# Sketched linear attention and a Fourier mixing block in one kernel: columns d and 128 - d folded before the row transform

## The chip, the cores and the metric

The kernel runs on one core of one Trainium2 chip. A core has five engines that work side by side: TensorE (PE in the profile; its weight loads are listed as PEld), VectorE (DVE), ScalarE (ACT), GpSimd (POOL) and SyncE (SP, which here only issues transfers, DMAs). The metric is the device time of one execution in microseconds. The profiler's records of one execution span a little less than that time; both are given below.

## The reference, cut to what matters

```python
# batch B = 4, heads H = 4, S = 1088 rows, D = 32, sketch R = 8, DM = H * D = 128
def phi(x):
    a = np.einsum('rd,bhsd->bhsr', S1, x)
    b = np.einsum('rd,bhsd->bhsr', S2, x)
    return np.einsum('bhsi,bhsj->bhsij', a, b).reshape(*x.shape[:-1], r * r)
q_p, k_p = (phi(q), phi(k))
kv = np.einsum('bhsf,bhsd->bhfd', k_p, v)
z = np.sum(k_p, axis=2)
num = np.einsum('bhsf,bhfd->bhsd', q_p, kv)
den = np.einsum('bhsf,bhf->bhs', q_p, z)[..., None] + 1e-06
x = (num / den)                       # then heads side by side: x is [4, 1088, 128]
X = np.fft.fft(x, axis=1)
X = np.fft.fft(X, axis=2)
u = x + np.real(X)
un = (u - mean(u)) / np.sqrt(var(u) + 1e-06)      # over the 128 columns
out = u + np.maximum(un @ w_ch1, 0.0) @ w_ch2     # w_ch1 [128, 512], w_ch2 [512, 128]
```

For the change only the middle matters: the real part of a two-dimensional Fourier transform, over the 1088 rows and then over the 128 columns. With cosine and sine tables C and S it is C x C - S x S.

## The kernel before, in words

The program is a list of named steps. Each step has one engine, a function that emits its instructions, and the things that it reads and writes. A string `ORDER` gives one sequence of all steps, so it fixes the order of every engine's own queue; `ENGINE` moves steps to another engine than their default; `BANK` gives each use of PSUM its bank (8 banks of 512 fp32); `BEHIND` makes a load wait until an earlier transfer has landed; `FILL` puts a number of products of zeros ahead of a PE step (three numbers: fp32 products, bf16 products, bank). Semaphores follow from what is read and written. Step names carry the batch b or the group g.

For each batch b:

- `qT`, `kT` (DVE): transposes of 32x32 blocks. `qf`, `kpr` (PE): sketches of q and k. `qa`, `kab` (ACT) copy one factor out of PSUM, `qp` (DVE) and `kp` (POOL or DVE) multiply. `vc` packs v with a column of ones.
- `kv` (PE, L339): sum over rows of features times v, 36 products that show as 72 instructions, because fp32 takes two passes; `kvz` copies it out. `pnd` (PE, L425): numerators and denominators, again 72 instructions. `den`, `rden` and `x` (DVE, L440) divide; x is written as bf16 in 9 blocks of 128 rows; block 8 holds the rows left over of both halves.
- `eo` (POOL or DVE, L96): sum and difference of rows s and s + 544, 128x512 bf16 each.
- `sC`, `sS` (PE, L453, L461, L462): the row transform with cosines and with sines. Each has 2 products of 273 columns for block 8 and 16 products of 136 or 137 columns; weights are all 128 columns of the folded x. `zC`, `zS` copy them out (128x546 each), `zrC`, `zrS` (128x544) make the mirrored half.
- `mix` (PE, L487, L492) for each half of the rows: u = x (one product with the identity) plus the column transform, for each of 4 blocks of 128 rows one product with the cosine matrix `cd` and one with the sine matrix `sd`. `mixl` (L498, L505) does the left-over rows of two batches, with 32-wide products.

Ten groups g follow (two halves of each batch, and two groups of left-over rows): `bn`, `var` (DVE), `sd` (ACT), `rc` (DVE), `un` give the normalized rows; `xt` is a transposing DMA on SP (groups 7, 8 and 9 use `tr` on PE and a copy `ut` instead); `ph` (PE, L559), `rl` (ACT L566 or DVE L568), `po` (PE, L573), `fin` and `out` are the two layers and the store. The left-over group is stored by four DMAs (`st_last`).

Before all that the tables are made: `c_...` constants, `t_turn`, `l_turn`, `d_turn` (POOL) and `t_ph`, `t_pm`, `l_ph`, `l_pm`, `d_ph`, `d_pm` (DVE) angles of the main table, of the left-over rows and of the columns; `t_sin`, `t_cos`, `l_...`, `d_trig` (ACT); `t_neg` the negated tables.

A product can use a part of the PE array. The profile prints that shape: 128\*128 is the whole array, 128\*64 a half of its columns, 128\*32 a quarter, 32\*64 an eighth.

Of the kernel before, what the change touches and what calls it, by code (L numbers as in the profile page):

```python
# [22 lines left out]
LAST = HALF - 512  # L23
NK = HALF // 2 + 1
NB = NK // 2 + 1
BY_DMA = (0, 1, 2, 3, 4, 5, 6)
TWO = 8
# [24 lines left out]
def program(nc, T, x, bank):  # L52
# [31 lines left out]
    def copy(engine, out, in_):  # L84
        if engine == ACTE:
            nc.scalar.copy(out, in_)  # L86
        elif engine == DVE:
            nc.vector.tensor_copy(out, in_)
        else:
            nc.gpsimd.tensor_copy(out, in_)  # L90

    def memset(engine, t, value):
        (nc.vector if engine == DVE else nc.gpsimd).memset(t, value)

    def tt(engine, out, in0, in1, op):
        (nc.vector if engine == DVE else nc.gpsimd).tensor_tensor(out=out, in0=in0, in1=in1, op=op)  # L96
# [32 lines left out]
    def ld_qt():  # L129
        return [nc.sync.dma_start(view(T("qt_in"), 0, [[D, B * H], [1, D]], 32 * j, 32),  # L130
                                  dram(x["q"], (512 + HALF * j) * D, [[D, 32], [S * D, B * H], [1, D]])) for j in range(2)]
# [41 lines left out]
    def c_rows():  # L173
        v = nc.vector
        pi, pa, sr = T("pi"), T("pa"), T("sr")
        v.tensor_scalar(out=pa[:, 0:1], in0=pi[:], scalar1=31, scalar2=None, op0=ALU.bitwise_and)  # L176
        v.tensor_scalar(out=pa[:, 1:2], in0=pi[:], scalar1=32, scalar2=None, op0=ALU.bitwise_and)
        v.tensor_scalar(out=sr[:, 5:6], in0=pa[:, 0:1], scalar1=512.0, scalar2=None, op0=ALU.add)
        v.tensor_scalar(out=sr[:, 4:5], in0=pa[:, 1:2], scalar1=HALF / 32.0, scalar2=sr[:, 5:6], op0=ALU.mult, op1=ALU.add)
        v.tensor_copy(sr[:, 5:6], pi[:])  # L180
        v.tensor_scalar(out=T("sq")[:, 0:5], in0=sr[:, 0:5], scalar1=1.0 / S, scalar2=None, op0=ALU.mult)
        v.tensor_scalar(out=T("sq")[:, 5:6], in0=sr[:, 5:6], scalar1=1.0 / DM, scalar2=None, op0=ALU.mult)
    add("c_rows", DVE, "iota", "rows", c_rows)

    def turn(ph, i, src, period):

        nc.gpsimd.tensor_scalar(out=ph, in0=src, scalar1=T("sq")[:, i:i + 1], scalar2=MAGIC, op0=ALU.mult, op1=ALU.add)
        nc.gpsimd.tensor_scalar(out=ph, in0=ph, scalar1=-MAGIC, scalar2=-float(period), op0=ALU.add, op1=ALU.mult)

    def rest(ph, i, src):  # L190
        nc.vector.scalar_tensor_tensor(out=ph, in0=src, scalar=T("sr")[:, i:i + 1], in1=ph, op0=ALU.mult, op1=ALU.add)  # L191

    def size(pm, ph):
        nc.vector.tensor_scalar(out=pm.bitcast(I32), in0=ph.bitcast(I32), scalar1=0x7FFFFFFF, scalar2=None, op0=ALU.bitwise_and)
# [42 lines left out]

    def d_trig():
        cos(T("cd")[:], T("dpm")[:], DM)
        sin(T("sd")[:, 0, :], T("dph")[:], DM, -1.0)  # L240
        sin(T("sd")[:, 1, :], T("dph")[:], DM)
    add("d_trig", ACTE, "dphb dpm hpi tabsin", "cd sd", d_trig)
# [65 lines left out]
    def kprod(engine, use, ab, kp, lo, hi):  # L308

        b = [[16, hi - lo], [0, R], [1, R]]  # L310
        tt(engine, view(kp, F * lo, [[F, hi - lo], [R, R], [1, R]]), ps(use, 16 * lo + R, b) if engine == DVE else view(ab, 16 * lo + R, b),
# [14 lines left out]
    def vcopy(b, engine):  # L326
        copy(engine, view(T(f"v{b % 2}"), 0, [[33, H], [33 * H, 8], [1, D]]), view(T(f"v_in{b % 2}"), 0, [[8 * D, H], [D, 8], [1, D]]))
# [116 lines left out]

    def fold(b, engine, w):
        tt(engine, T(f"eo{b % 2}")[:, w], T(f"x{b}")[:, 0:4, :], T(f"x{b}")[:, 4:8, :], (ALU.add, ALU.subtract)[w])

    def srow(b, trig):

        ahead = ((0, -3, -4, 7), (1, 2, -5, -6))[trig]  # L450
        z = f"z{trig}{b}"
        for c in range(2):
            nc.tensor.matmul(ps(z, 512 * c, [[1, NK]]), T(f"x{b}")[:, 8, :], T("tabl")[:, trig, NK * c:NK * c + NK],  # L453
                             start=True, stop=False, skip_group_check=True)
        for c in range(2):
            for t in range(4):
                w = T(f"eo{b % 2}")[:, c, t, :]
                i = ahead[t]
                m = T("tab")[:, 2 * t + trig, NB * c:NB * c + NB - c]
                far = T("tab")[:, i, NB * c + 1 - c:NB * c + NB - c] if i >= 0 else T("neg")[:, -i - 3, NB * c + 1 - c:NB * c + NB - c]  # L460
                nc.tensor.matmul(ps(z, 512 * c, [[1, NB - c]]), w, m, start=False, stop=(t == 3), skip_group_check=True)  # L461
                nc.tensor.matmul(ps(z, 512 * c + NB - c, [[1, NB - 1]]), w, far, start=False, stop=(t == 3),  # L462
                                 skip_group_check=True)

    def zev(b, trig, engine):
        copy(engine, view(T(f"z{b}"), 2 * NK * trig, [[1, 2], [2, NK]]), ps(f"z{trig}{b}", 0, [[512, 2], [1, NK]]))

    def zrev(b, trig, engine):
        copy(engine, view(T(f"zr{b}"), 2 * NK * trig, [[1, HALF]]), view(T(f"z{b}"), 2 * NK * trig + HALF, [[-1, HALF]]))


    def zcol(b, trig, half, first, step, n):

        return view(T(f"z{b}" if half == 0 else f"zr{b}"), 2 * NK * trig + first, [[step, n]])
# [8 lines left out]
    def mix(b, half, g):  # L483
# [5 lines left out]
        for t in range(4):  # L489
            for trig in range(2):  # L490
                w = T("cd")[:] if trig == 0 else T("sd")[:, half, :]
                nc.tensor.matmul(ps(u, ut_at(g, t), [[1, 128]]), zcol(b, trig, half, t, 4, 128), w, start=False, stop=True,  # L492
                                 skip_group_check=True)

    def mixl(i):
# [4 lines left out]
        for b in (2 * i, 2 * i + 1):  # L500
            for half in range(2):
                for trig in range(2):
                    w = T("cd")[:] if trig == 0 else T("sd")[:, half, :]
                    p = 64 * (b % 2) + 32 * half
                    nc.tensor.matmul(ps(u, 0, [[1, 128]], p, 32), zcol(b, trig, half, 512, 1, LAST), w, start=False, stop=True,  # L505
                                     tile_position=(0, p), skip_group_check=True)
# [5 lines left out]
    def var(g, n, engine):  # L512
# [8 lines left out]
        p.tensor_tensor(out=d, in0=st[:, 0:n, 1], in1=st[:, 0:n, 4], op=ALU.subtract)  # L521
# [3 lines left out]
        p.tensor_tensor(out=v, in0=v, in1=d, op=ALU.add)  # L525

# [60 lines left out]
    def st_last(i, g):  # L587
        return [nc.sync.dma_start(dram(x["out"], ((2 * i + j // 2) * S + 512 + HALF * (j % 2)) * DM, [[DM, 32], [1, DM]]),
                                  T(f"ot{g % 4}")[32 * j:32 * j + 32, 0:128]) for j in range(4)]
# [38 lines left out]
    for b in range(B):  # L628
# [12 lines left out]
        for w in range(2):  # L641
            e = eng(f"eo{b}.{w}", POOL)
            add(f"eo{b}.{w}", e, f"x:{b}", f"eo:{b}/{w}", lambda b=b, w=w, e=e: fold(b, e, w))
        for trig, n in ((0, "C"), (1, "S")):
            add(f"s{n}{b}", PE, f"eo:{b}/0 eo:{b}/1 x:{b} tab/S0 tab/S1 tab/C0 tab/C1 neg tabL/{n}",
                f"pz{n}:{b}", lambda b=b, trig=trig: srow(b, trig), f"z{trig}{b}:2")
            e = eng(f"z{n}{b}", ACTE)
            add(f"z{n}{b}", e, f"pz{n}:{b}", f"z{n}:{b}", lambda b=b, trig=trig, e=e: zev(b, trig, e), f"z{trig}{b}:2")
            e = eng(f"zr{n}{b}", POOL)
            add(f"zr{n}{b}", e, f"z{n}:{b}", f"zr{n}:{b}", lambda b=b, trig=trig, e=e: zrev(b, trig, e))  # L650
        for half in range(2):
            mixer(b, half, g, (f"zC:{b} zS:{b}", f"zrC:{b} zrS:{b}")[half] + f" x:{b} idb cd sd")
# [11 lines left out]
    "kk": ([128, 2 * NK], FP32), "pi": ([128, 1], I32), "pa": ([128, 2], I32),  # L664
# [4 lines left out]
    "cd": ([128, DM], BF16), "sd": ([128, 2, DM], BF16),  # L669
# [11 lines left out]
    "x": (4, [128, 9, DM], BF16), "eo": (2, [128, 2, 4, DM], BF16), "z": (4, [128, 2, 2 * NK], BF16), "zr": (4, [128, 2, 2 * NK], BF16),  # L681
# [6 lines left out]
def kernel(  # L688
# [108 lines left out]
```

## Time and profile before

| what | value |
|---|---|
| median of 3 runs | 88.58 us (87.52 to 89.68) |
| time of the profiled execution | 87.8 us |
| span of its records | 86.0 us |
| mean granted TensorE clock | 0.969 |
| busy: PE, DVE, ACT, POOL | 76.1, 63.4, 52.5, 41.0 us |
| moved by DMA | 10.49 MB |

A row of a timeline reads: start and duration in us, engine, line, operation, output <- inputs, shape in the PE array (for PE), shapes of the operands, how many instructions in a row; in brackets the idle time before it and what ended it. Matmuls are pipelined and their ends are modelled, so products overlap in the list; the distance between two starts is what a product costs. A row of groups reads: busy us, mean ns of one, then idle time before them. A row of stages reads: busy us of each engine with the number of its instructions, then the granted clock, the share of the DMA engines and GB/s.

### The profile page before, as it was taken

What the parts mean: (1) busy time and instruction counts of PE and PEld (TensorE: products, weight loads), DVE (VectorE), ACT (ScalarE), POOL (GpSimd) and SP (SyncE); (2) the same over time, 40 slices, a digit from 0 to 9 for tenths busy, and PEclk for the clock granted to TensorE, in tenths of its full rate; (3) what the DMA queues carried; (4) which work ended last, traced back from release to release, by engine and by line L of the source; (5) the groups of instructions that cost most, each with busy time, mean ns of one, the idle gap of its engine ahead of it and who ended that gap; (6) DMA issues with size and microseconds to landing.
All of it is one profiled execution on the core that took longest, in us unless ns stands there. A gap on an engine that the chain in (4) does not pass through costs nothing.

```text
span 86.0 us, 3396 instructions
## 1 busy us (share of the span) xinstructions
PE 76.1 (89%) x1434; PEld 58.1 (68%) x1442; DVE 63.4 (74%) x168; ACT 52.5 (61%) x91; POOL 41.0 (48%) x57
## 2 busy tenths in 40 slices
PE   0999999991999999999999999999999988979530
PEld 0244556791899776879799797987777965757220
DVE  5699999999956999975793577395989537682710
ACT  3413669926826535668966176639659859899510
POOL 7888659997076730499992328037500220000000
PEclk9999999999759999999999999999999999999995
DMA  0889996599687862400003001133060360251413
GB/s 4 226 241 326 272 228 115 161 247 294 218 214 209 278 175 58 134 0 8 0 11 61 0 8 30 39 61 126 1 189 0 76 183 0 71 206 75 182 34 119
DMA packets 16176, 10.49 MB, mean 122 GB/s; under 512 B 6944, under 2 KB 14624, under 8 KB 16160
## 3 DMA queue, kind: packets, MB, share of 16 engines
q1 hardware_dynamic: 15976, 10.13, 42.2%
q8 instruction: 11, 0.18, 0.9%
q10 hardware_dynamic: 184, 0.14, 0.5%
q14 instruction: 5, 0.04, 0.1%
HBM read 7.22 MB, written 2.23 MB: 110 GB/s over the span
## 4 chain that ended last, share of the span: by engine, by line
PE 66%; DVE 23%; issue 3%; ACT 3%; POOL 1%
PE ps L425 12%; PE ps L573 9%; PE ps L339 8%; PE ps L559 7%; PE ps L379 6%; PE ps L492 5%; PE ps L462 4%; PE ps L461 4%; DVE t_ph L191 4%; PE ps L453 3%; PE ps L305 3%; ACT t_ht__158 L566 2%; PE ps L487 2%; DVE t_qT__116 L372 1%; DVE t_ht__157 L568 1%
## 5 line engine op out<-in xcount | busy, mean ns | idle before, releaser
L566 ACT ACTIVATE t_ht__158<-ps 128x1024 bf16<-128x1024 f32 x8 | 8.1, 1023 | 1.8 <-PE ps L462 1.1
L96 POOL TENSOR_TENSOR t_kp__119<-t_ab__117 128x512 f32<-128x512 f32 x6 | 6.3, 1068 | 6.1 <-ACT t_ab__117 L357 6.1
L96 POOL TENSOR_TENSOR t_kp__120<-t_ab__118 128x512 f32<-128x512 f32 x8 | 8.9, 1143 | 0.0
L566 ACT ACTIVATE t_ht__157<-ps 128x1024 bf16<-128x1024 f32 (+1 forms) x7 | 6.7, 962 | 2.0 <-PE ps L559 1.9
L78 PE MATMUL ps<-t_wz 128*128 128x512 f32 x6 | 4.3, 810 | 2.0 <-DVE t_pa L176 2.0
L573 PEld LDWEIGHTS <-t_ht__157 128*128 128x128 bf16 x68 | 3.9, 98 | 2.6 <-DVE t_ht__157 L568 1.1
L573 PE MATMUL ps<-t_w2b,t_ht__157 128*128 128x128 bf16 x68 | 4.8, 220 | 0.9 <-DVE t_ht__157 L568 0.9
L425 PE MATMUL ps<-t_kvz,t_qp__125 128*64 128x66 f32 x128 | 5.5, 261 | 0.0
L425 PEld LDWEIGHTS ps<-t_kvz,t_qp__125 128*64 128x64 f32 x128 | 5.2, 173 | 0.5 <-issue 0.4
L386 ACT COPY t_qa__124<-ps 128x1024 f32<-128x1024 f32 x4 | 4.1, 1013 | 1.9 <-PE ps L379 1.4
L573 PE MATMUL ps<-t_w2b,t_ht__158 128*128 128x128 bf16 x68 | 4.8, 219 | 0.3 <-ACT t_ht__158 L566 0.3
L573 PEld LDWEIGHTS <-t_ht__158 128*128 128x128 bf16 x68 | 4.1, 98 | 1.4 <-DVE t_ht__158 L568 0.5
L386 ACT COPY t_qa__123<-ps 128x1024 f32<-128x1024 f32 x4 | 4.0, 1004 | 1.1 <-PE ps L379 1.1
L90 POOL COPY t_zr__142<-t_z__138 128x544 bf16<-128x544 bf16 x2 | 1.3, 642 | 7.1 <-ACT t_z__138 L86 5.6
L223 POOL TENSOR_SCALAR t_neg<-t_tab 128x1096 bf16<-128x1096 bf16 x1 | 3.0, 3001 | 3.2 <-ACT t_tab L200 3.2
L339 PEld LDWEIGHTS ps<-t_v__122,t_kp__120 128*64 128x64 f32 x128 | 4.2, 141 | 0.4 <-issue 0.4
L379 PE MATMUL ps<-t_qT__116,t_sa 32*64 32x256 f32 x64 | 2.8, 400 | 1.9 <-DVE t_qp__126 L390 1.9
L425 PEld LDWEIGHTS ps<-t_kvz,t_qp__126 128*64 128x64 f32 x128 | 3.9, 137 | 0.8 <-issue 0.8
L339 PEld LDWEIGHTS ps<-t_v__121,t_kp__119 128*64 128x64 f32 x128 | 4.1, 138 | 0.6 <-POOL t_zr__139 L90 0.4
L339 PE MATMUL ps<-t_v__122,t_kp__120 128*64 128x33 f32 x128 | 4.4, 225 | 0.0
L339 PE MATMUL ps<-t_v__121,t_kp__119 128*64 128x33 f32 x128 | 4.3, 224 | 0.0
L461 PE MATMUL ps<-t_tab,t_eo__133 128*128 128x137 bf16 (+1 forms) x32 | 4.3, 223 | 0.0
(257 smaller groups left out, 237.5 us busy)
## 6 DMA issues: line engine op xcount, KB each, us to landing
t_q_in__110<-in_q_dram SPq DMA_DIRECT2D x4, 256.0 KB, 3.4
t_k_in__107<-in_k_dram SPq DMA_DIRECT2D x2, 512.0 KB, 4.6
t_v_in__108<-in_v_dram SPq DMA_DIRECT2D x8, 128.0 KB, 3.4
t_v_in__109<-in_v_dram SPq DMA_DIRECT2D x8, 128.0 KB, 3.4
t_k_in__106<-in_k_dram SPq DMA_DIRECT2D x2, 256.0 KB, 4.7
t_q_in__111<-in_q_dram SPq DMA_DIRECT2D x2, 256.0 KB
t_q_in__112<-in_q_dram SPq DMA_DIRECT2D x2, 256.0 KB
t_k_in__106<-in_k_dram SPq DMA_DIRECT2D x1, 512.0 KB, 5.3
```

Source lines behind the costliest of these rows:

```text
L78: nc.tensor.matmul(T("ps")[:, free, :], T("wz")[:, 0:128], T("wz")[:], start=True, stop=True)
L96: (nc.vector if engine == DVE else nc.gpsimd).tensor_tensor(out=out, in0=in0, in1=in1, op=op)
L191: nc.vector.scalar_tensor_tensor(out=ph, in0=src, scalar=T("sr")[:, i:i + 1], in1=ph, op0=ALU.mult, op1=ALU.add)
L339: nc.tensor.matmul(ps(f"kv{b}", 33 * pr, [[1, 33]], 64 * c, 64), kp, v, start=(t == 0), stop=(t == 8), tile_position=(0, 64 * c), skip_gro ...
L379: nc.tensor.matmul(ps(f"q{b}.{pr}", 512 * g + 256 * w, [[1, 256]], 64 * h, 64), view(T(src), 0, [[1, F]], 32 * g, 32), view(T(f"qT{b % 2}" ...
L386: nc.scalar.copy(T(f"qa{pr}")[:], ps(f"q{b}.{pr}", 0, [[512, 4], [1, 256]]))
L425: nc.tensor.matmul(ps(f"nd{b}", 512 * (s // 3) + 132 * (s % 3) + 66 * pr, [[1, 66]], 64 * c, 64), w, view(T("kvz"), 132 * b + 66 * pr, [[1 ...
L461: nc.tensor.matmul(ps(z, 512 * c, [[1, NB - c]]), w, m, start=False, stop=(t == 3), skip_group_check=True)
L492: nc.tensor.matmul(ps(u, ut_at(g, t), [[1, 128]]), zcol(b, trig, half, t, 4, 128), w, start=False, stop=True, skip_group_check=True)
L559: nc.tensor.matmul(ps(use, 128 * n * i, [[1, 128 * n]]), T("w1b")[:, 128 * c:128 * c + 128], T(f"unT{g % 3}")[:, 0:128 * n], start=True, s ...
L566: nc.scalar.activation(out=out, in_=in_, func=ACT.Relu)
L573: nc.tensor.matmul(ps(u, ut_at(g, t), [[1, 128]]), T(f"ht{g % 2}")[:, c, 128 * t:128 * t + 128], T("w2b")[:, c, :], start=False, stop=True ...
```

## The change

Columns d and 128 - d of x have the same cosine and opposite sines. The new steps `df{b}.0` and `df{b}.1` write `xd`, for each of the 9 blocks 129 columns: the 64 even ones (columns 0 to 63, of which 1 to 63 are sums), then 64 odd ones (a zero and 63 differences), then column 64. The step `eo` works on `xd` instead of x. One step `s{b}` takes the place of `sC` and `sS`: the even columns are multiplied by cosines, the odd ones by sines, in the two halves of the PE array, and column 64 by cosines in a product with one column of weights. Results of both lie in one bank pair, so one step `z` copies them out; `zr` makes the mirrored half with a sign per partition; a new step `zl` collects the left-over rows, which are now ordered by parity. The column transform needs one product per block, with a matrix `wd` that holds both cosines and sines.

`xd` has one buffer. `ENGINE`, `FILL`, `BEHIND`, `ORDER` and `BANK` are all new, and a table `AFTER` lets a step wait for another one that it doesn't depend on. `qt_in` is loaded by 4 DMAs of 16 rows instead of 2 of 32, and a left-over group is stored by 8 DMAs instead of 4.

```diff
+    def dfold(b, engine, w):
+
+        X, Y = T(f"x{b}"), T(f"xd{b % NXD}")
+        n = 2 * QD + 1
+        if w == 0:
+            copy(engine, view(Y, 0, [[n, 9], [2 * QD, 2]]), view(X, 0, [[DM, 9], [QD, 2]]))
+        return tt(engine, view(Y, QD * w + 1, [[n, 9], [1, QD - 1]]), view(X, 1, [[DM, 9], [1, QD - 1]]),
+                  view(X, DM - 1, [[DM, 9], [-1, QD - 1]]), (ALU.add, ALU.subtract)[w])
+
     def fold(b, engine, w):
-        tt(engine, T(f"eo{b % 2}")[:, w], T(f"x{b}")[:, 0:4, :], T(f"x{b}")[:, 4:8, :], (ALU.add, ALU.subtract)[w])
-
-    def srow(b, trig):
+        return tt(engine, T(f"eo{b % 2}")[:, w], T(f"xd{b % NXD}")[:, 0:4, :], T(f"xd{b % NXD}")[:, 4:8, :], (ALU.add, ALU.subtract)[w])
+
+    def srow(b):
+
+
+        def product(c, part, w, mov, off, n, start, stop):
+            p = QD * (c ^ (part > 0))
+            lo, m = ((0, QD), (QD, QD), (2 * QD, 1))[part]
+            nc.tensor.matmul(ps(f"z{b}", 512 * c + off, [[1, n]], p, m), w[:, lo:lo + m], mov, start=start, stop=stop,
+                             tile_position=(0, p), skip_group_check=True)
+
+        def six(weights, movs, offs, ns, start, stop):
+
+            for c, part in ((0, 0), (0, 1), (1, 2), (0, 2), (1, 1), (1, 0)) if not start else ((0, 0), (0, 1), (1, 1), (1, 0), (1, 2), (0, 2)):
+                product(c, part, weights[c], movs[c][part == 1], offs[c], ns[c], start and part < 2, stop)
+        tabl = T("tabl")
+        six([T(f"xd{b % NXD}")[:, 8, :]] * 2, [[tabl[:, trig, NK * c:NK * c + NK] for trig in range(2)] for c in range(2)],
+            (0, 0), (NK, NK), True, False)
...
+        for t in range(4):
...
+            six(w, [[T("tab")[:, 2 * t + trig, NB * c:NB * c + NB - c] for trig in range(2)] for c in range(2)],
+                (0, 0), (NB, NB - 1), False, t == 3)
...
+            six(w, far, (NB, NB - 1), (NB - 1, NB - 1), False, t == 3)
+
+    def zev(b, engine):
+        copy(engine, view(T(f"z{b}"), 0, [[1, 2], [2, NK]]), ps(f"z{b}", 0, [[512, 2], [1, NK]]))
...
         for t in range(4):
-            for trig in range(2):
-                w = T("cd")[:] if trig == 0 else T("sd")[:, half, :]
-                nc.tensor.matmul(ps(u, ut_at(g, t), [[1, 128]]), zcol(b, trig, half, t, 4, 128), w, start=False, stop=True,
-                                 skip_group_check=True)
+            nc.tensor.matmul(ps(u, ut_at(g, t), [[1, 128]]), view(T(("z", "zr")[half] + str(b)), t, [[4, 128]]), T("wd")[:, t % 2, :],
+                             start=False, stop=True, skip_group_check=True)
...
+AFTER = {
+    "t_turn0": "t_ph1", "l_turn": "d_ph", "kp0.2": "d_pm", "kp1.1": "t_pm1", "d_alt": "l_pm", "vc2": "t_neg", "eo2.1":
+    "df2.0",
+}
```

The new order of PE's steps around the row transforms is: `kv0 pnd0 kv1 qf2.1 pnd1 w1c qf3.1 kpr2 s0 qf2.0 kpr3 mix0 kv2 qf3.0 mix1 s1 pnd2 ph0.1 kv3 mix2 ph0.0 pnd3 s2 mix3 ph1.0 ph1.1 po0 ph2.0 ph2.1 mix5 po1 po2 ph3.1 mix4 mix6 ph3.0 s3 po3 ph5.1 mix7 ph4.0 ph5.0 po4 tr7 ph6.1 ph6.0 mix9 po5 ph7.0 ph7.1 po6 mix8 tr9 po7 ph9.0 po9 tr8 ph8.1 ph8.0 po8.0 po8.1`. Before it was `qf1.1 pnd0 kv1 qf2.1 pnd1 w1c qf3.1 kpr2 sC0 kpr3 qf2.0 sS0 sS1 mix0 qf3.0 kv2 sC1 mix1 pnd2 ph0.1 kv3 mix2 ph0.0 pnd3 sC2 po0 ph1.1 mix3 ph1.0 sS2 ph2.0 po1 ph2.1 mix5 mix4 po2 ph3.1 ph3.0 mix6 sC3 po3 sS3 ph5.0 ph4.0 mix7 ph5.1 po4 ph6.1 po5 ph6.0 tr7 mix8 ph7.0 mix9 ph7.1 po6 tr8 tr9 po7 ph9.0 ph8.1 ph8.0 po9 po8.0 po8.1`.

On DVE `l_ph` and `l_pm` now stand behind `qp1.0`, `qp1.1` and `qT2`, ahead of `rden0`; `t_neg` is on DVE behind `x1`; `df2.0`, `df2.1` and `eo2.0` are on DVE, the other folds on POOL. `FILL` has entries for `s_t qf0.1 kpr0.1 qf0.0 qf1.0 pnd0 ph5.0 tr7 po9 ph8.1`.

## The prediction, made blind

> **What bounds the kernel now.** I read the page first, its busy times, slices and chain.
>
> ```profile
> span 86.0 us, 3396 instructions
> PE 76.1 (89%) x1434; PEld 58.1 (68%) x1442; DVE 63.4 (74%) x168; ACT 52.5 (61%) x91; POOL 41.0 (48%) x57
> PE   0999999991999999999999999999999988979530
> PEclk9999999999759999999999999999999999999995
> PE 66%; DVE 23%; issue 3%; ACT 3%; POOL 1%
> ```
>
> PE is full from about 21 to 70 us, except for a hole near 20 us, behind which its clock falls for two slices. The DVE part of the chain lies before that hole. The stages say the same, and the PE timeline shows the hole's cause:
>
> ```profile
> 10.00:20.00 10.00, 9.09 (x232) 6.96 (x230) 10.00 (x13) 5.97 (x10) 8.72 (x10) 1.00 0.87 199
> 30.00:40.00 10.00, 10.00 (x231) 7.88 (x226) 8.49 (x11) 5.77 (x9) 5.19 (x6) 1.00 0.29 81
> 70.00:80.00 10.00, 9.10 (x106) 6.33 (x107) 6.08 (x28) 9.21 (x16) 0.64 (x1) 1.00 0.32 105
> 21.24 0.69 PE L379 MATMUL ps<-t_qT__116,t_sa 32*64 32x256 f32 x16 [1.94 <-DVE t_qp__126 L390]
> ```
>
> So a microsecond of PE work between 21 and 70 us is worth nearly a microsecond, if nothing else takes PE's place. Then I asked the PE timeline what one product costs, and what a change of shape in the array costs:
>
> ```profile
> 35.80 0.22 PE L461 MATMUL ps<-t_tab,t_eo__133 128*128 128x136 bf16 x1
> 35.86 0.22 PE L462 MATMUL ps<-t_tab,t_eo__133 128*128 128x136 bf16 x1
> 36.01 0.39 PE L305 MATMUL ps<-t_sblk,t_kT__114 128*64 128x64 f32 x6
> ...
> 62.52 0.22 PE L498 MATMUL ps<-t_x__129,t_idb 128*128 128x128 bf16 x1
> 62.58 0.22 PE L498 MATMUL ps<-t_x__130,t_idb 128*128 128x128 bf16 x1
> 62.73 0.23 PE L505 MATMUL ps<-t_cd,t_z__135 128*32 128x128 bf16 x1
> ...
> 62.75 0.23 PE L505 MATMUL ps<-t_cd,t_zr__140 128*32 128x128 bf16 x1
> 62.80 0.22 PE L505 MATMUL ps<-t_sd,t_z__135 128*32 128x128 bf16 x1
> ...
> 62.81 0.22 PE L505 MATMUL ps<-t_sd,t_zr__140 128*32 128x128 bf16 x1
> 62.97 0.29 PE L573 MATMUL ps<-t_w2b,t_ht__157 128*128 128x128 bf16 x2
> ```
>
> Two things to see. Products in different column strips run together: four start from 62.73 to 62.75, the next four at 62.80, after one stream of 128 columns. And where the shape changes, 0.06 from start to start becomes 0.15 or 0.16 (35.86 to 36.01, 62.58 to 62.73, 62.81 to 62.97). All 16 changes behind streams of up to 137 columns show it: 149 to 156 ns, so 0.09 us for a change.
>
> **The row transform.** Before, a batch takes 2.5 us: sC0 from 34.71 to 36.01 is 1.30, sS0 and sS1 from 38.15 to 40.56 are 2.41. After it is 9 groups of six products, in three pairs; each pair runs side by side in two column halves. Streams: 3 x 0.12 for the 273-column pairs (L453 starts 0.12 apart) and 24 x 0.06, with 0.15 to leave: 1.95 us. But two of each six have one weight column. The narrowest form in the trace is 128\*32, and I take them to run as that; then each group goes from 128\*64 to 128\*32 and back. That is 18 changes per batch, 18 x 0.09 = 1.6, so 3.5 us. No row shows a change between these two shapes, so the bounds are 1.95 (free) and 3.9 (each change as seen, and 0.04 more for the second pair behind it, as L425 starts at 29.27, 29.37, 29.43). I take 3.5, since every change seen costs the same and the second set of 32-wide products shows no such extra. Over four batches: **+4.0 us** (from -2.2 to +5.6).
>
> [...]
>
> **The column transform.** mix was 0.22 for the identity and 8 x 0.056; it loses 4 x 0.056, eight times: 1.8. mixl loses one of its two sets of four, 0.06, twice. **-1.9 us**, all on PE; between 0 (at the end, where PE waits anyway) and -1.9.
>
> **Copies and mirrors.** One z of 0.79 instead of two per batch. zr is two of 272 instead of two of 544 (0.64 each on POOL), now scaled: by the POOL rows of 274 fp32 (0.43 to 0.58), about 1.0 against 1.3. zl adds two small ones (0.2). They lie beside PE work: mix1 stands two steps of 3.3 us behind mix0, zr0 needs 1.9. If that cover goes, b = 3 pays first, because zr3 and zl3 precede mix9; there POOL has little else.
>
> **The folds.** These lie between x and the row transform. POOL does 512 bf16 in 1.16 to 1.35 us:
>
> ```profile
> L96 POOL TENSOR_TENSOR t_eo__133<-t_x__129 128x512 bf16<-128x512 bf16 x2 | 2.3, 1168 | 1.3 <-DVE t_x__129 L440 1.3
> L96 POOL TENSOR_TENSOR t_eo__134<-t_x__130 128x512 bf16<-128x512 bf16 x1 | 1.3, 1347 | 0.0
> ```
>
> So 567 cost 1.3 to 1.5, two of them and a copy of 18 elements 2.9 a batch. For b = 0: x0 at 27.8 (below), folds until 33.1; PE reaches s0 at 33.6: hidden by 0.5. For b = 1 POOL also has vc2, kp2.2, kp2.0; vc2 now waits (AFTER) for t_neg, some 1.0 us, and all that stands behind it on POOL waits with it. eo1.1 ends at 43.1, PE comes to s1 at 43.4 because s0 is long; with s0 at 1.95 PE would wait 0.9. For b = 2 DVE folds: pnd2 ends at 49.4, then den, rden, zl1, x2 (2.3), two folds at 0.91 x 567/512 = 1.0, bn2 0.9, var2 0.4 and eo2.0 0.9: 55.7 against PE at 55.2. **+0.5 us** (0 to 1). For b = 3 the folds take 6 us behind the start of s2, and PE has over 8 us until s3. The second wait, for the single xd, is met by then in each case.
>
> [...]
>
> **The beginning.** Table work of 4.8 us (DVE 15.31 to 20.05: L191, L191, L194, L191) stood ahead of qp1.0, and PE waited until 21.24. After, qp1.0 comes at about 16.7, and kv0 waits for POOL (kp0, t_turn2, kt_p: about 18) and for the last small v load: SP issues ld_qt as 4 x 0.52, and kt, q1, k1 and six loads stand between, so it lands near 18. kv0 2.2, kvz0 0.5, pnd0 2.3: pnd0 ends at 23.4 instead of 26.18. But l_ph and l_pm (2.2) now stand ahead of rden0, so x0 ends at 27.8 (before: 28.39), and pnd1, which shares banks with pnd0, waits for it. qp2.1 and qf3.1 follow DVE; kpr2 ends at 33.6, where before sC0 began at 34.78. **-1.2 us**, between 0 (loads late) and -2.7 (pnd0's whole lead). d_alt (eight memsets, 1.0) is ahead of df0 on POOL, but waits only for l_pm at 26 and is done before x0. The other AFTER waits fall in POOL's idle start.
>
> **Between and the end.** With ph1.0 and ph1.1 together, ACT does rl1.0, sd3, rl1.1 in line and ph2.1 waits; ph3.1 waits for xt3: **+0.6** (0 to 1.5). From the start of the last copy of z, po3 0.9, ph5.1 0.4, mix7 0.45, bn7, var7, sd7, rc7, un7 2.4 with handovers, tr7 0.2, ph6 0.9, mix9 0.25, po5 0.9, ph7 0.9, po6 0.9: mix8 starts 8.4 later. From there mix8 0.45, bn8 to un8 2.4, tr8 0.23, ut8 0.42, ph8.1 0.45, rl8.1 1.23, po8 0.9, fin8.1 0.37, the last 3.1 (82.89 to 86.0) and 0.8 of handovers; 0.4 more, because SP issues eight stores of 0.49 for out9 ahead of out8.0: 10.4. 18.8 against 16.75 before, of which po3 (0.9) only moved: **+1.1** (-1 to +2). The fills (pnd0, ph5.0, tr7, po9, ph8.1: 11 x 0.215) lie in PE's waits for kvz0, rl5.1, un7, rl9 and ut8; uncovered they would cost 2.4.
>
> **The sum.** 87.8 + 4.0 - 1.9 + 0.5 - 1.2 + 0.6 + 1.1 = **90.9 us**. It is made against the profiled execution, 87.8 (1.8 beyond its span of 86.0), which is 0.8 below the median of the three, 88.58.
>
> **Rivals.**
> - *The one-column products cost no change of shape.* 6.2 us less on PE, 0.9 back in the wait for eo1.1: 85.6, faster. It decides from the price of a change: 72 of them carry the 3.1 us that I forecast, so below 0.09 - 0.043 = 0.047 us the kernel is no slower. For it: both shapes split the array in columns, and no row shows a switch between them. Against: every switch seen costs 0.09.
> [...]
> - *The folds run at half that speed on POOL*, because one operand runs backwards from an odd element. Then s0 starts 2.3 later and s1 another 2.5: 95.7. Against: POOL's rows go by elements (0.64 for a copy of 544 bf16, 1.1 for 512 fp32 products).
>
> **How the numbers follow.** Forecast 0.63 (its own range 89.3 to 92.8, from the bounds of the beginning, the waits and the end), no change of shape 0.16, half a drain 0.17, slow folds 0.04. The range from 87.3 to 94.0 holds the forecast's cases and the half drain, and leaves out the free changes and the slow folds, 0.20. Within 2% is about what a measurement of this kernel can tell from no change. Faster: 0.16. Same: the half drain and the forecast's lower end, 0.27. Slower: 0.57.
>
> **What would show it.** In the PE timeline of the new row transform: the shape printed for the one-column products, and 0.15 us from the last start of one shape to the first of the next; a batch of 3.5 us. mix without half of its L492 products. df groups on POOL of 1.3 to 1.5. pnd0 ending near 23.4 at full clock, x0 near 27.8. From the last z to the end 18 to 19 us. Row transforms of 2 us a batch would make the prediction wrong.

## The result, and the profile after

The changed kernel takes 93.50 us, median of 4 runs (92.59 to 96.82), beside 88.05 us for the kernel before (86.93 to 89.68, 4 runs): the ratio is 1.068, with a 95% interval of 1.051 to 1.086. Timed once more on another chip it was 93.13 us (92.99 to 93.25) beside 88.34, ratio 1.070 (1.062 to 1.077). The forecast was 90.9 us. Ratios leave out runs with a disturbed clock (such as the 96.82), so they can differ a little from the quotient of two medians; beside the experiments the kernel before took 86.2 to 87.5 us where its mean granted clock was 0.99 or more, and 87.5 to 89.9 us where it was lower.

The profiled execution took 93.26 us, with a span of 91.5. Its page, the lines that answer to those shown of before:

```profile
span 91.5 us, 3521 instructions
PE 80.4 (88%) x1474; PEld 54.2 (59%) x1484; DVE 63.8 (70%) x177; ACT 50.4 (55%) x93; POOL 45.5 (50%) x76
PE   3999997998999999999999999998499988998440
PEclk9999999999999999999999999999999999999995
PE 46%; DMA 24%; DVE 9%; SPq 9%; ACT 5%; issue 2%; DVEq 0%
```

PE's busy time went up by 4.3 us (76.1 to 80.4) although each `mix` lost four of its nine products. The hole near 20 us is gone, and so are the two slices of a lower clock; no run shows that the hole was their cause. The row transform's line, L486, alone holds 17% of the chain. Its end of the first batch, in the PE timeline:

```profile
36.20 0.31 PE L486 MATMUL ps<-t_tab,t_eo__134 128*64 128x136 bf16 x3
36.29 0.23 PE L486 MATMUL ps<-t_neg,t_eo__134 128*64 128x136 bf16 x1
36.45 0.23 PE L486 MATMUL ps<-t_tab,t_eo__134 128*1 128x136 bf16 x2
36.60 0.25 PE L486 MATMUL ps<-t_neg,t_eo__134 128*64 128x136 bf16 x1
36.61 0.25 PE L486 MATMUL ps<-t_tab,t_eo__134 128*64 128x136 bf16 x1
36.78 0.69 PE L402 MATMUL ps<-t_qT__115,t_sa 32*64 32x256 f32 x16
```

The one-column products are printed as 128\*1, a shape of their own, and not as 128\*32. (Whether the array treats them as it treats 128\*32 stays open: no run has a change between these two.) From the last pair of halves to the pair of one-column products is 0.16 (36.29 to 36.45), and back 0.15 (36.45 to 36.60). A second pair of halves behind a change comes 0.08 to 0.09 later (36.20 to 36.29), and not 0.06. By the starts of L486 and of the product behind it, the four batches take 3.83 (32.95 to 36.78), 3.76, 3.84 and 3.86 us: 3.82 on average.

Further down, in the PE timeline, the holes ahead of the last row transform, and the queue of SP at that place:

```profile
62.23 0.59 PE L610 MATMUL ps<-t_unT__161,t_w1b 128*128 128x512 bf16 x2 [0.39 <-ACT t_ht__163 L617]
...
66.31 0.38 PE L610 MATMUL ps<-t_unT__159,t_w1b 128*128 128x512 bf16 x1 [1.21 <-DMA t_unT__159<-t_un__156]
...
68.09 0.64 PE L486 MATMUL ps<-t_tabl,t_xd__133 128*64 128x273 bf16 x6
```

```profile
62.27 1.19 SPq L602 DMA_TRANSPOSE t_unT__159<-t_un__156  x1
63.55 0.53 SPq L635 DMA_DIRECT2D out_dram<-t_ot__164  x1
64.85 0.36 SPq L635 DMA_DIRECT2D out_dram<-t_ot__165  x1
66.04 1.20 SPq L602 DMA_TRANSPOSE t_unT__161<-t_un__158  x1
```

ph3.1 starts at 66.31, 4.0 us after its transposing transfer xt3 was issued (62.27). PE stands for 1.21 us ahead of it; with the 0.39 ahead of ph2.1 and another 0.12 that is 1.7 us.

The new small operations, from the groups of POOL and of DVE:

```profile
L95 POOL TENSOR_TENSOR t_xd__133<-t_x__129 128x567 bf16<-128x567 bf16 x2 | 2.5, 1266 | 0.0
L516 POOL TENSOR_SCALAR t_zr__142<-t_z__138,t_sgn 128x272 bf16<-128x272 bf16 x2 | 2.0, 1051 | 0.0
```

```profile
L95 DVE TENSOR_TENSOR t_xd__133<-t_x__131 128x567 bf16<-128x567 bf16 x2 | 0.9, 458 | 0.1
L95 DVE TENSOR_TENSOR t_eo__134<-t_xd__133 128x516 bf16<-128x516 bf16 x1 | 0.4, 398 | 0.0
```

A fold of 567 elements costs POOL 1.27 us and DVE 0.46. The mirror with a sign per partition costs POOL 1.05 us for only 272 elements.

### The profile page after: what moved, and what is told of

Read it like the earlier page. It is cut to its first block, busy times and chain, and to the rows that moved or that the text cites. A ratio compares the mean times of both kernels' runs of the same rounds, so it can differ in the third digit from the quotient of the medians.

```text
span 91.5 us, 3521 instructions
## 1 busy us (share of the span) xinstructions
PE 80.4 (88%) x1474; PEld 54.2 (59%) x1484; DVE 63.8 (70%) x177; ACT 50.4 (55%) x93; POOL 45.5 (50%) x76
## 4 chain that ended last, share of the span: by engine, by line
PE 46%; DMA 24%; DVE 9%; SPq 9%; ACT 5%; issue 2%; DVEq 0%
PE ps L486 17%; DMA t_q_in__112<-in_q_dram 6%; DMA t_k_in__106<-in_k_dram 6%; PE ps L362 5%; PE ps L448 5%; PE ps L610 5%; DMA t_unT__159<-t_un__156 4%; PE ps L624 4%; DMA t_q_in__110<-in_q_dram 4%; PE ps L402 4%; DMA t_qt_in<-in_q_dram 3%; SPq L118 3%; ACT t_ht__163 L617 3%; PE ps L328 2%; SPq L112 2%
## 5 line engine op out<-in xcount | busy, mean ns | idle before, releaser
L617 ACT ACTIVATE t_ht__163<-ps 128x1024 bf16<-128x1024 f32 (+1 forms) x8 | 7.8, 970 | 5.9 <-DVE t_st__151 L560 4.4
L617 ACT ACTIVATE t_ht__162<-ps 128x1024 bf16<-128x1024 f32 (+1 forms) x6 | 5.7, 955 | 3.1 <-PE ps L610 2.6
L82 PE MATMUL ps<-t_wz 128*128 128x512 bf16 x20 | 6.9, 431 | 0.2 <-issue 0.2
L95 POOL TENSOR_TENSOR t_kp__119<-t_ab__117 128x512 f32<-128x512 f32 x6 | 6.2, 1070 | 1.3 <-DVE t_dpm L198 1.3
L95 POOL TENSOR_TENSOR t_kp__120<-t_ab__118 128x512 f32<-128x512 f32 x6 | 6.2, 1065 | 0.9 <-DVE t_pm L198 0.9
L95 POOL TENSOR_TENSOR t_eo__134<-t_xd__133 128x516 bf16<-128x516 bf16 x3 | 3.1, 1047 | 7.1 <-DVE t_xd__133 L95 7.0
L486 PE MATMUL ps<-t_tab,t_eo__135 128*64 128x136 bf16 (+2 forms) x72 | 6.1, 232 | 0.0
L486 PE MATMUL ps<-t_tab,t_eo__134 128*64 128x136 bf16 (+2 forms) x72 | 6.1, 232 | 0.0
L610 PEld LDWEIGHTS <-t_w1b 128*128 128x128 bf16 x40 | 3.3, 97 | 4.3 <-issue 3.1
L486 PEld LDWEIGHTS <-t_eo__135 128*64 128x64 bf16 (+1 forms) x96 | 3.7, 98 | 3.0
L486 PEld LDWEIGHTS <-t_eo__134 128*64 128x64 bf16 (+1 forms) x96 | 3.7, 98 | 3.0
L624 PEld LDWEIGHTS <-t_ht__162 128*128 128x128 bf16 x68 | 4.0, 98 | 2.5 <-ACT t_ht__162 L617 2.0
L362 PE MATMUL ps<-t_v__122,t_kp__120 128*64 128x33 f32 x128 | 4.4, 223 | 0.3
L362 PEld LDWEIGHTS ps<-t_v__122,t_kp__120 128*64 128x64 f32 x128 | 4.1, 138 | 0.7 <-issue 0.7
```

What stands on the lines that cost most here:

```text
L82: nc.tensor.matmul(T("ps")[:, free, :], w[:, 0:128], w[:, 0:512], start=True, stop=True)
L95: return (nc.vector if engine == DVE else nc.gpsimd).tensor_tensor(out=out, in0=in0, in1=in1, op=op)
L362: nc.tensor.matmul(ps(f"kv{b}", 33 * pr, [[1, 33]], 64 * c, 64), kp, v, start=(t == 0), stop=(t == 8), tile_position=(0, 64 * c), skip_gro ...
L486: nc.tensor.matmul(ps(f"z{b}", 512 * c + off, [[1, n]], p, m), w[:, lo:lo + m], mov, start=start, stop=stop, tile_position=(0, p), skip_gr ...
L610: nc.tensor.matmul(ps(use, 128 * n * i, [[1, 128 * n]]), T("w1b")[:, 128 * c:128 * c + 128], T(f"unT{g % 3}")[:, 0:128 * n], start=True, s ...
L617: nc.scalar.activation(out=out, in_=in_, func=ACT.Relu)
```

## The experiments

**The theories for the row transform.** A: the time is set by the number of changes between the shapes 128\*64 and 128\*1, 18 in a batch. B: the two column halves don't run side by side, or the one-column products are slow in themselves; then the number of changes doesn't matter, the number of products does. C: the row transform is hidden or not by what follows, and the new order of issue, not PE's work, sets the end. The first four runs keep all else and vary only the products of column 64. Beside them the kernel before took 88.67 us (86.18 to 89.81, 7 runs).

**One change per batch.** The 18 one-column products come behind the 36 others.

```diff
+            for c, part in ((0, 0), (0, 1), (1, 1), (1, 0)):
+                product(c, part, weights[c], movs[c][part == 1], offs[c], ns[c], start, stop)
+            late.extend((c, 2, weights[c], movs[c][0], offs[c], ns[c], False, stop) for c in (1, 0))
...
+        for a in late:
+            product(*a)
```

> The kernel after, with the same 54 products for each row transform, but the 18 with one column of weights behind the 36 others: one change of array shape inside instead of 18. Theory A (a change of shape costs 0.10 us, 72 of them are what made the row transforms 3.8 us): a row transform takes 0.24 + 33 x 0.06 fewer waits, about 2.05 us, PE loses 4 x 1.75 = 7 us; some of it comes back as waits for the folds of batch 1 and in the tail, so 87.5 us (86.3 to 89.5). Rival B (the two column halves don't run side by side, 54 products at 0.07): row transform stays 3.8, time 93.3. Rival C (the new order of steps, not the row transform, sets the end): row transform 2.05, but the time stays above 92.

Measured: 86.05 us (85.37 to 87.19). The PE timeline of its first batch, at the seam:

```profile
33.20 0.22 PE L486 MATMUL ps<-t_tab,t_eo__134 128*64 128x136 bf16 x1
33.35 0.28 PE L486 MATMUL ps<-t_tabl,t_xd__133 128*1 128x273 bf16 x2
33.47 0.34 PE L486 MATMUL ps<-t_tab,t_eo__134 128*1 128x136 bf16 x6
33.65 0.22 PE L486 MATMUL ps<-t_neg,t_eo__134 128*1 128x136 bf16 x2
33.71 0.23 PE L486 MATMUL ps<-t_tab,t_eo__134 128*1 128x136 bf16 x2
33.77 0.23 PE L486 MATMUL ps<-t_neg,t_eo__134 128*1 128x136 bf16 x2
33.83 0.29 PE L486 MATMUL ps<-t_tab,t_eo__134 128*1 128x136 bf16 x4
34.05 0.47 PE L402 MATMUL ps<-t_qT__115,t_sa 32*64 32x256 f32 x8
```

Two one-column products take 0.06 together (33.71, 33.77, 33.83), the same as a pair of halves. They are not slow in themselves; the only place inside the batch with 0.15 is the seam at 33.20 to 33.35. A batch took 2.00, 2.02, 2.06 and 2.01 us, with all 54 products (behind the third PE waits another 0.21 for x3, which isn't counted). So B falls.

**Half of the changes.** Groups of six alternate: the one-column products come last in one group and first in the next, which leaves 9 changes a batch.

```diff
+            order = ((0, 0), (0, 1), (1, 1), (1, 0), (1, 2), (0, 2)) if count[0] % 2 == 0 else ((1, 2), (0, 2), (1, 1), (1, 0), (0, 0), (0, 1))
```

> The kernel after, the same products, but one-column products stand last in one group of six and first in the next: 9 or 10 changes of shape in a row transform instead of 18. A: 0.10 for each change that is gone, so 3.8 - 0.85 = 2.95 us a batch and about 90 us. B: 3.8 us, 93.3. C: 2.95 us, but above 92.

Measured: 89.67 us (88.84 to 90.78), batches of 2.86, 2.88, 2.86 and 2.89 us.

**No change.** 63 columns of zeros behind column 64 in `xd` and `eo`, so that its products have 64 columns of weights, like the others. The zeros are written once, by three memsets on POOL.

```diff
+    def c_pad():
+        for t in (T("xd0"), T("eo0"), T("eo1")):
+            nc.gpsimd.memset(t[:, :, 2 * QD + 1:3 * QD] if len(t.shape) == 3 else t[:, :, :, 2 * QD + 1:3 * QD], 0.0)
...
-            lo, m = ((0, QD), (QD, QD), (2 * QD, 1))[part]
+            lo, m = ((0, QD), (QD, QD), (2 * QD, QD))[part]
```

> The kernel after, with 63 columns of zeros behind column 64 in the folded x, so that the one-column products get 64 columns of weights and the shape of the others: no change of shape inside, the stream of columns is the same, weight loads are longer. One memset of the zeros is added on GpSimd in an idle stretch. A: 1.95 to 2.1 us a batch, time as with the one-column products last, 87.5 (86.3 to 89.5). B: 3.8 and 93.3. If long weight loads are what costs: over 2.5 us a batch.

Measured: 85.32 us (84.63 to 86.94). The end of its first batch in the PE timeline:

```profile
33.16 0.22 PE L492 MATMUL ps<-t_neg,t_eo__134 128*64 128x136 bf16 x1
33.21 0.23 PE L492 MATMUL ps<-t_tab,t_eo__134 128*64 128x136 bf16 x2
33.28 0.22 PE L492 MATMUL ps<-t_neg,t_eo__134 128*64 128x136 bf16 x1
33.28 0.23 PE L492 MATMUL ps<-t_tab,t_eo__134 128*64 128x136 bf16 x1
33.44 0.47 PE L407 MATMUL ps<-t_qT__115,t_sa 32*64 32x256 f32 x8
```

The same 54 products, a pair every 0.06, and one change, to the sketch that follows (33.28 to 33.44). Three batches take 1.90 to 1.94 us (31.52 to 33.44 the first). Behind the third PE waits 0.29 for x3, so the next product starts 2.27 after the batch did, as it does in the runs with one change and without column 64. That column 64 now goes with 64 weights instead of one costs nothing: a pair takes 0.06 either way.

**Without column 64.** Its 18 products a batch are left out, so the transform lacks that column's share; 36 products remain.

```diff
-            for c, part in ((0, 0), (0, 1), (1, 2), (0, 2), (1, 1), (1, 0)) if not start else ((0, 0), (0, 1), (1, 1), (1, 0), (1, 2), (0, 2)):
+            for c, part in ((0, 0), (0, 1), (1, 1), (1, 0)):
```

> The kernel after without the products of column 64, so without that column's part of the transform: 36 products in one shape. A: 0.24 + 16 x 0.06 + exit 0.15 = 1.35 us a batch, 2.45 less each; with the waits for folds that then show 86 to 88 us. B: 36 x 0.07 = 2.5 us a batch and 93.3 - 5 = 88.3, as much for each product left out as a product costs. C: above 91.

Measured: 84.25 us (83.43 to 84.66), about 1.4 us of PE work a batch; with the waits behind three of them the next product starts 1.52, 1.96, 2.27 and 1.32 us after the batch did. So the shorter batches mostly turn into waits, and the time is below the padded version's for another reason, which comes further down (xt3). Together, with such waits left out of the second column:

| products, changes of shape in a batch | a batch, us | median, us |
|---|---|---|
| 54, 18 (the change) | 3.82 | 93.50 |
| 54, 9 | 2.87 | 89.67 |
| 54, 1 | 2.02 | 86.05 |
| 54, 0 (padded) | 1.92 | 85.32 |
| 36, 0 | 1.4 | 84.25 |

Per change that is (3.82 - 1.92) / 18 = 0.106 us, (2.87 - 1.92) / 9 = 0.106, and 0.10 for the single one: the price is nearly the same at every dose, and A stands. On the whole kernel 72 changes are 7.6 us by that price. The medians differ by 8.2, but they come from separate measurements; on one chip (below) it is 7.2. From the start of s0 to the end of the records the change takes 58.5 and 58.7 us in its two traces, the padded version 51.5 and 51.4. So nearly all of the row transform's time comes back, less the 0.3 that PE now waits for x3, and C falls. The medians of the first, third and fourth run lie below the ranges expected for them (which began at 86.3, 86.3 and 86), since those had let more of the gain go into new waits.

**What the late part waits for.** The next four runs start from the padded version, since there PE's own work hides less. Beside them the kernel before took 87.88 us (86.3 to 89.91, 7 runs). Three suspects: the products of zeros (`FILL`) in the last stage; S, that the stores issued on SP delay the transposing transfers; O, that tr7, which waits for un7, holds up the products of group 6 behind it on PE.

Without the products of zeros ahead of ph5.0, tr7, po9 and ph8.1:

```diff
-    5), "ph5.0": (0, 1, 1), "tr7": (0, 3, 1), "po9": (0, 3, 3), "ph8.1": (0, 2, 3),
+    5),
```

> The padded kernel (no change of shape in the row transforms, 85.3 us) without the products of zeros ahead of ph5.0, tr7, po9 and ph8.1. If they lie in waits, as the prediction says: 85.3, within 0.3, the same starts of the steps behind them, and the granted clock still 1 up to 80 us. If they stand in the way: up to 2.2 us less. If they hold the clock up: the products behind them get longer, 86 or more.

Measured: 86.06 us (85.27 to 86.46). Where they had been, PE has holes instead (0.98 us ahead of tr7, 0.75 ahead of po9, 0.52 ahead of ph8.1). They lay in waits and cost nothing: from the start of s3 to the end of the records it is 21.43 us, against 21.45 in the padded version, and the granted clock stays at 0.9 or more in every slice but the last, as in the padded version. The median came out 0.7 above the expected 85.3; in the traces s0 starts later (32.97 against 31.52), ahead of anything that the edit touches.

The first two stores moved behind the transposing transfer xt5 on SP:

```diff
-fin0 mix5 rl2.0 po1 rl2.1 po2 fin1 xt3 out0 ph3.1 bn5 var5 sd5 rc5 fin2 zr2 eo3.0 out1 mix4 rl3.1 mix6 un5 bn4 var4
-sd4 ph3.0 s3 rl3.0 po3 xt5 out2 bn6 ...
+fin0 mix5 rl2.0 po1 rl2.1 po2 fin1 xt3 ph3.1 bn5 var5 sd5 rc5 fin2 zr2 eo3.0 mix4 rl3.1 mix6 un5 bn4 var4
+sd4 ph3.0 s3 rl3.0 po3 xt5 out0 out1 out2 bn6 ...
```

> The padded kernel with the stores out0 and out1 issued behind the transposing transfer xt5 instead of right behind xt3. The hole of 1.2 us on PE ahead of ph3.1 waits for xt3, which took 4.0 us there. Theory S (a store of 256 KB issued behind it slows the transposing transfer): xt3 lands after 2.4 us, the hole shrinks to 0.1, s3 starts 1.1 earlier, 84.2 us; ph5.1 may wait for xt5 instead. Rival (the transfer is as slow by itself there, or the wait is for something else): the hole stays, 85.3.

Measured: 85.37 us (85.18 to 88.23). Its SP queue, and the product that waits for the transfer, in the PE timeline:

```profile
56.53 1.19 SPq L608 DMA_TRANSPOSE t_unT__159<-t_un__156  x1
60.30 1.19 SPq L608 DMA_TRANSPOSE t_unT__161<-t_un__158  x1
61.58 0.53 SPq L641 DMA_DIRECT2D out_dram<-t_ot__164  x1
```

```profile
60.55 0.59 PE L616 MATMUL ps<-t_unT__159,t_w1b 128*128 128x512 bf16 x2 [1.19 <-DMA t_unT__159<-t_un__156]
```

With nothing issued behind it on SP for 2.6 us, the transfer still takes 4.0 us from its issue to the product (56.53 to 60.55), and the hole is 1.19. S falls.

But such a transfer doesn't need 4.0 us by itself. The four others of this shape whose landing this trace holds land 2.4 us after their issue; before, it was 2.3 to 2.4. In the run without column 64 so does xt3, with a store issued behind it as in the change, and ph3.1 doesn't wait. Its SP queue and its product:

```profile
55.90 1.19 SPq L602 DMA_TRANSPOSE t_unT__159<-t_un__156  x1
57.19 0.53 SPq L635 DMA_DIRECT2D out_dram<-t_ot__164  x1
```

```profile
58.56 0.59 PE L610 MATMUL ps<-t_unT__159,t_w1b 128*128 128x512 bf16 x2
```

The times to landing for this buffer, in the padded version and then in the run without column 64:

```profile
DMA to landing us min/median/max: 2.4/3.2/4.0
DMA to landing us min/median/max: 2.4/2.4/2.4
```

What differs is one packet of 16,384 bytes on the queue that the page lists as "q8 instruction". With the stores moved it lasts from 58.41 to 59.43 us. All but six of xt3's own small packets have started by 58.56; the last six start at 59.41 to 59.56. In all eleven traces in which such a packet starts 1.9 to 2.1 us after the issue of xt3, xt3 lands after 4.0 to 4.2 us; in the run without column 64 the next one starts at 61.67, long after. No run moved that packet alone, so this is read from the traces and not tried.

tr7 and its copy moved behind ph6:

```diff
-ph5.0 po4 sd7 rc7 un7 fin4 rl5.0 zr3 zl3 tr7 ut7 ph6.1 out4 ph6.0 rl6.1 rl6.0 mix9 ...
+ph5.0 po4 sd7 rc7 un7 fin4 rl5.0 zr3 zl3 ph6.1 out4 ph6.0 tr7 ut7 rl6.1 rl6.0 mix9 ...
```

> The padded kernel with tr7 and ut7 behind ph6.0 instead of ahead of ph6.1. Theory O (the new order makes the tail long, since PE's queue stands at tr7 until un7 is done): the two products of ph6 move 0.9 us forward, rl6, po6 and mix8 follow in part, 84.7 us (84.4 to 85.1). Rival (the tail is a chain through ACT and DVE that tr7 doesn't hold up): 85.3.

Measured: 86.69 us (86.17 to 88.39). The PE timeline:

```profile
67.02 0.59 PE L616 MATMUL ps<-t_unT__159,t_w1b 128*128 128x512 bf16 x2
68.46 0.59 PE L616 MATMUL ps<-t_unT__159,t_w1b 128*128 128x512 bf16 x2 [0.85 <-ACT t_ht__163 L623]
...
70.51 0.22 PE L556 MATMUL ps<-t_x__131,t_idb 128*128 128x128 bf16 x1 [0.58 <-DVE t_unT__160 L89]
```

The group that was to fill the wait for un7 waits itself, in the middle (0.85, for ACT) and ahead of mix9 (0.58, for the copy ut7): one wait has become two. From s3 to the end it takes 22.72 us instead of 21.45, slower than both expectations had it. O falls.

All three edits together:

> The padded kernel with the three edits together: late fills left out, stores behind the transposes, tr7 behind ph6. If S and O hold: 83.6 us. If neither: 85.3.

Measured: 86.74 us (86.08 to 87.1). No gain, as from each alone, and 1.4 above the 85.3 expected for that case. Since s0 starts anywhere from 31.5 to 33.3 us, the medians of these runs are less steady than the stretches behind it:

| run | from s2 to s3, us | from s3 to the end of the records, us |
|---|---|---|
| the change | 12.95 | 23.38 |
| padded, two traces | 11.38, 11.38 | 21.45, 21.46 |
| without the late products of zeros | 11.36 | 21.43 |
| stores moved | 11.34 | 21.45 |
| tr7 moved | 11.40 | 22.72 |
| all three | 11.41 | 22.04 |
| without column 64 | 10.01 | 21.93 |

In these stretches the change is 1.57 and 1.93 us longer than the padded version, which is what its third and fourth batch take more (3.84 - 2.27 and 3.86 - 1.94). The run without column 64 gains 1.37 from s2 to s3, where its third batch ends no earlier: that is the wait for xt3.

**Work in the hole.** If PE only stands there because ph3.1 is issued too early, the products of mix6 and mix4, which follow it, can go ahead of it. This ran beside the padded version and the change as it is, on one chip (before: 88.34 us, 86.55 to 89.87, 11 runs).

```diff
-... xt3 out0 ph3.1 bn5 var5 sd5 rc5 fin2 zr2 eo3.0 out1 mix4 rl3.1 mix6 un5 bn4 ...
+... xt3 out0 bn5 var5 sd5 rc5 fin2 zr2 eo3.0 out1 mix6 mix4 ph3.1 rl3.1 un5 bn4 ...
```

> The padded version with mix6 and mix4 issued on PE ahead of ph3.1 instead of behind it. If the transposing transfer xt3 needs 4.0 us from its issue by itself, ph3.1 keeps its start (issue of xt3 plus 4.0, near 59.8) and mix6 (0.45) and mix4 (0.38) lie in the hole of 1.23 ahead of it: the hole is cut to about 0.4, s3 starts about 0.8 us earlier, and the time is 0.5 to 0.8 below the padded version's. If the wait belongs to something that moves with PE's order (the banks or the later steps), ph3.1 moves back by 0.8 and nothing is gained.

> The padded version once more, on the chip of the others: near 85.3 us, some 3% below the kernel before, if every product of the row transform in the one shape 128*64 is what was missing; row transforms of 1.92 us.

> The changed kernel as it is, on the chip of the others: near 93.3 us, 8 above the padded version. By the theory of changes of shape 72 changes at 0.104 us are 7.5 us of it.

Measured: 86.17 us (85.82 to 87.65) with the mixes ahead, ratio to before 0.989 (0.982 to 0.996); 85.93 (85.2 to 86.02) for the padded version, ratio 0.986 (0.979 to 0.992); 93.13 for the change as it is. Padding alone takes 7.2 us off the change here, and leaves a kernel 1.4% below the one before: real by its interval, but under 2%. The PE timeline of the run with the mixes ahead, then ACT's:

```profile
60.00 0.38 PE L547 MATMUL ps<-t_x__131,t_idb 128*128 128x512 bf16 x1 [0.67 <-ACT t_ot__166 L88]
...
60.81 1.04 PE L616 MATMUL ps<-t_unT__159,t_w1b 128*128 128x512 bf16 x4
62.59 0.54 PE L492 MATMUL ps<-t_tabl,t_xd__133 128*64 128x273 bf16 x6 [0.74 <-ACT t_ht__163 L623]
```

```profile
61.52 1.02 ACT L623 ACTIVATE t_ht__163<-ps 128x1024 bf16<-128x1024 f32 x1 [1.57 <-PE ps L616]
```

That expectation failed. The hole ahead of ph3.1 is filled, but the first of the moved products waits 0.67 itself, for a copy on ACT, so ph3.1 starts 0.3 us after xt3 has landed (60.81, and 56.50 + 4.02), and a new hole of 0.74 opens behind it. s3 takes the bank of h3.1 (`z3=0`, `h3.1=0`), so it waits until rl3.1 on ACT has emptied it: rl3.1 runs from 61.52 to 62.54, and s3 starts at 62.59. The same holds in the padded version and in the change as it was made:

```profile
67.00 1.02 ACT L617 ACTIVATE t_ht__163<-ps 128x1024 bf16<-128x1024 f32 x1 [1.28 <-remote]
```

There rl3.1 ends at 68.02 and s3 starts at 68.09. So ahead of the last row transform the chain is xt3 (4.0 here), ph3.1 (0.7 to the activation), rl3.1 (1.0), s3. From the issue of xt3 to s3 it is 5.8 us in the change and in the padded version, 6.1 with the mixes ahead, and 4.5 without column 64, where xt3 landed after 2.4. Moving the mixes inside that stretch changed only where PE's idle time shows.

## Why the prediction was right about the sign and wrong about the size

The forecast was +3.1 us over the profiled 87.8; the profiled execution after shows +5.5. The steps, as the prediction summed them:

| term | forecast, us | measured, us |
|---|---|---|
| row transform | +4.0 | +5.6 |
| column transform | -1.9 | -1.8 |
| folds | +0.5 | 0 |
| beginning | -1.2 | -1.8 |
| between | +0.6 | +1.7 |
| end | +1.1 | +1.8 |
| sum | +3.1 | +5.5 |

The measured entries are read from the starts in the two profiled executions.

**Row transform: the step that failed, by its size.** The mechanism was right: changes of shape between the halves and the one-column products, 18 a batch, at the price seen elsewhere. The prediction took 3.5 us against 2.5 before, at 0.09 a change, and argued that the second pair behind a change shows no extra. It measured 3.82 against 2.43 (the blocks of before add up to 9.73 us for the four batches), so +5.6. The trace after and the padded one give the price, from the start of one pair to the start of the next, behind streams of 136 or 137 columns:

| step | us |
|---|---|
| no change | 0.061 |
| into the one-column products | 0.161 |
| back to the halves | 0.154 |
| second pair of halves behind a change | 0.084 |

A batch has 9 changes each way and 7 such second pairs: 9 x 0.100 + 9 x 0.093 + 7 x 0.023 = 1.90, and the padded 1.92 makes it 3.82. Over the four batches the second pairs are 0.65 us of the 1.6 by which the term fell short, the changes themselves 0.35, the rounding of 1.95 + 18 x 0.09 = 3.57 down to 3.5 another 0.3, and 2.5 taken for 2.43 the last 0.3. The upper bound of 3.9 had put 0.04 on the second pair, by the rows of L425; the truth lay half-way, and the forecast went with the row of the 32-wide products that showed nothing. (The 16 changes that it counted leave out two early ones of 0.20 us, to the products at 5.75 and 17.01.) The first rival (no price, 85.6 us) was wrong for this kernel; its number is what the padded version, which has no such change, then gave: 85.3 to 85.9. That is partly luck, since the other terms of its sum were off too. The case of half the price at each change (72 x 0.045 = 3.2 us less, 87.7 us), which the chances call half a drain, fell with the 0.15 from start to start. No run shows a drain of the array; what the runs show is 0.106 us a change all told, 3.82 against 1.92 over 18 changes.

The trace after shows the price between products printed as 128\*64 and as 128\*1, for which the trace of before had no row: 0.161 us in and 0.154 back, where pairs of one shape start 0.061 apart.

**Between.** Its bounds were 0 to 1.5, and 1.7 came. The prediction saw that ph3.1 waits for xt3, but counted it as one late product. 1.21 of the 1.7 lie ahead of ph3.1, because xt3 landed 4.0 us after its issue, where those of before took 2.4. PE was free at 65.10; an estimate from the issue at 62.27 and the usual 2.4 lets xt3 land at 64.7, with no wait. So most of this miss goes with the instruction packet that falls on xt3 in both traces of the change. The trace of before, where every landing that it holds for such a transfer is 2.3 to 2.4, could not show it. Behind xt3 the runs showed a chain through an activation and a PSUM bank, on which PE's order had no hold.

**The end.** From the last copy of z (72.06) to the end is 19.4 us, forecast 18.8. mix8 starts 8.6 behind that copy (forecast 8.4), and the rest takes 10.8 (10.4). No single step failed: the items that the prediction lists add up to 8.2 and 10.75, which it wrote as 8.4 and 10.4. Against before, less the 0.9 of po3 that only moved, it is +1.8 (19.4 - 16.75 - 0.9). Moving tr7 cost 1.3 us, and the fills lie in waits, as the prediction had them.

**The folds.** On POOL they cost 1.26 us (forecast 1.3 to 1.5), so the rival of slow folds fell, and s0 never waits. For b = 2 the prediction let DVE take 1.0 a fold, by a row of 0.91 beside POOL work; they took 0.46, and eo2.0 took 0.40 where 0.9 was forecast. POOL was idle during these folds (on DVE from 51.47 to 52.39 and from 53.74 to 54.14; POOL has no instruction from 45.53 to 52.54 and from 53.59 to 57.53), while it was busy in that row of before (on DVE from 35.99 to 36.90; on POOL from 35.56 to 38.95). Whether that is the reason no run tried.

**The beginning.** As forecast, the hole near 20 us went, and pnd0 ended at 23.85 (forecast 23.4):

```profile
21.52 2.09 PE L448 MATMUL ps<-t_kvz,t_qp__125 128*64 128x66 f32 x64 [0.34 <-ACT t_kvz L88]
23.42 0.43 PE L448 MATMUL ps<-t_kvz,t_qtp 128*64 128x66 f32 x8
```

In the profiled execution of before, pnd0 had run from 22.29 to 26.18 at a lower clock (the value behind the busy times is the granted clock):

```profile
20.00:30.00 10.00, 8.76 (x232) 7.81 (x234) 7.99 (x12) 6.16 (x12) 5.51 (x4) 0.83 0.82 240
```

After, the clock of the same stretch is 1.00, so part of this lead exists only against an execution whose clock fell. l_ph and l_pm cost less of the lead than forecast, 0.75 and 0.45 us (23.22 and 24.00 on DVE) instead of 2.2: x0 was done at 26.2 instead of 27.8, and s0 starts at 32.95 where sC0 had started at 34.71. In the other runs s0 starts at 31.5 to 33.3, so this term is known to about 1 us only.

**The column transform** was right:

```profile
52.01 0.39 PE L541 MATMUL ps<-t_x__130,t_idb 128*128 128x512 bf16 x1
52.23 0.39 PE L544 MATMUL ps<-t_wd,t_z__137 128*128 128x128 bf16 x4
52.46 0.38 PE L610 MATMUL ps<-t_unT__159,t_w1b 128*128 128x512 bf16 x1
```

mix takes 0.45 (52.01 to 52.46) instead of 0.67, eight times.

## What to carry to other kernels

Count the changes of shape in the array, not only the products: here the folded row transform would have gained 2.0 us, 4 x (2.43 - 1.92), and 72 changes at 0.106 us made it lose 5.6; padding the one-column products to the shape of their neighbours, or issuing them together, gave that back. A price that is multiplied by 72 needs its third decimal, so look for every row that shows it, the second product behind a change too. Before moving work into a hole on PE, follow the chain beyond the product behind the hole: here the next stage's PSUM bank was still held for an activation, and the idle time only moved. And compare a slow transfer with others of its shape before taking its time for a price: xt3 took 4.0 us where they took 2.4.

## What the runs showed of the hardware that had not been expected

- Products with one column of weights are printed as a shape of their own (128\*1); a change from 128\*64 to them takes 0.161 us from start to start, and back 0.154. Two of them in different halves run together in 0.06 us, like products with 64 columns.
- Behind a change of shape to the halves the second pair starts 0.084 us after the first, instead of 0.061 (28 of 28). Behind a change to the one-column products it starts after 0.06 as ever (12 of 12, in the run with half of the changes).
- A tensor_scalar on POOL with a scalar per partition, read backwards at a step of 2, took 1.05 us for 272 bf16 elements; the plain copy of 544 before took 0.64.
- A transposing transfer of 128x512 bf16 between on-chip buffers landed 2.3 to 2.6 us after its issue, with a store issued behind it or without. When an instruction packet of 16,384 bytes (0.9 to 1.0 us long) started 1.9 to 2.1 us after the issue, among the transfer's own last packets, it landed after 4.0 to 4.2 us (eleven traces); in one case the packet lay 0.6 to 1.6 us after the issue, and the transfer landed after 3.1.
